# Softmax denominators of a fused attention and MoE kernel: block sums on VectorE and a 20-column product in place of a full-width product, with a newly searched order on TensorE

## The chip, the cores and the metric

The kernel runs on one core of one Trainium2 chip. TensorE (PE) multiplies, VectorE (DVE), ScalarE (ACT) and GpSimd (POOL) do the elementwise work, SyncE (SP) issues the transfers. The metric is device time in microseconds (us), the median of the runs; lower is better.

## The reference

Two stages. The first is attention with queries averaged in pairs, for 8 batches and 8 heads; its output, rearranged to 576 rows of 512 for each batch, goes into a mixture of four causal attention experts of which each row takes two.

```python
# stage 1: q, k, v are (8, 8, 1152, 64)
q_pool = q.reshape(B, H, S // 2, 2, D).mean(axis=3)
scores = scale * np.matmul(q_pool, k.transpose(0, 1, 3, 2))
attn = np.exp(scores - np.max(scores, axis=-1, keepdims=True))
attn = attn / (np.sum(attn, axis=-1, keepdims=True) + 1e-09)
attn_out = np.matmul(attn, v)
# stage 2: x is (8, 576, 512), for each of E = 4 experts, K = 2 chosen for each row
q, k, v = x @ wq[e], x @ wk[e], x @ wv[e]
scores = np.where(causal, -1e9, scale * (q @ k.transpose(0, 2, 1)))
a = np.exp(scores - scores.max(-1, keepdims=True))
a /= a.sum(-1, keepdims=True) + 1e-09
ye = a @ v @ wo[e]                # out += gate weight of (row, e) * ye
```

Both stages divide by a sum of P = exp(scores - max) over the keys. That sum is what the change touches.

## The kernel before

The 64 heads are taken in 32 pairs p, two heads side by side in 128 partitions (`HEAD[0]`, `HEAD[1]`). The 576 pooled queries of a pair are cut into two blocks of 256 and 320 (`QB`), the 1152 keys into nine chunks of 128. Scores are computed transposed: keys in the partitions, queries along the columns, so that P (`pt`, 128 x 2 heads x up to 320) is at once the right operand of the product with V.

TensorE's work comes in three kinds, each a way of splitting the array:

- A (`rows2`, line L326): two products of 64 rows each at once. The scores in four terms (qh, kh; qh, kl; ql, kh; RM, ON), and the plain products whose row maximum DVE takes (`row_max`, L573; tile PM).
- B (`cols2`, L333): two products of 64 output columns each at once, fp32. P times V into an accumulator, and the denominators. The trace keeps two records for each fp32 matmul, so one call of `cols2` is four records.
- C (`mm`, L317, and the transposes of L623): the whole array. The projections of the experts (x with WH, WL), the output product (y with OH, OL), and small ones.

The sum over the keys runs in two steps. ACT copies the first chunk's P into `sacc` (`act_first`, L342), POOL adds the other chunks elementwise (`pool_tt`, L350). What is left is a sum over 128 partitions. Before the change `g_norm` leaves it to TensorE: `cols2` with a 128 x 64 matrix of ones as the left operand writes `den`, 64 identical rows of n = 256 or 320 sums for each head. DVE then transposes `den` in 32 x 32 blocks into `rd` (L723), takes the reciprocal of one column of each block (L726, 8 or 10 numbers for each partition), multiplies by the gate weight in the expert stage (L732), and spreads the numbers back along the columns with a second block transpose (L735). `g_split` then scales the accumulator with it and splits the result into a high and a low part for the next product. There are 96 such products: 64 in stage 1 (32 pairs, two blocks), 32 in the expert stage (8 batches, two pairs of experts, two blocks).

`sacc` comes from a ring of three buffers (`NSA`), `pt` from one of 11, and all results of TensorE (scores, accumulators, `den`) from eight PSUM banks (`gen`).

The order in which instructions stand on the engines is set when the kernel is built. A planner keeps a clock for each engine, with a cost for each instruction (`emit`), and at each step takes the next piece of work from a set of generators (`f_max`, `f_st`, `f_av`, `g_norm` and others). How it chooses is steered by a row of 13 numbers out of the table `PLAN`, one row for each half pair: how long it may wait for work of the kind that is running, from which rank work is put off, how many products with V must be ready before kind B is entered, and so on. Before the change the table is 16 rows, then 8 rows five times over, then 9 rows. A generator's condition `rdy("DVE", t)` offers a step to DVE only when DVE's clock has reached the time t at which its input is due; `on(...)` gives TensorE the time itself.

Of the kernel before, what the change touches and what calls it, by code (L numbers as in the profile page):

```python
# [60 lines left out]
HEAD = [  # L61
# [16 lines left out]
]  # L78
CYCLE = [
# [8 lines left out]
]  # L88
TAIL = [
# [9 lines left out]
]  # L99
PLAN = HEAD + CYCLE * 5 + TAIL  # L100
# [61 lines left out]
def pooled_attention_then_moe_kernel(ctx: ExitStack, tc: tile.TileContext, qT, kT, vP, wall, wop, out):  # L162
# [25 lines left out]
    ones = cst.tile([128, 64], F32, name="ones")  # L188
    nc.vector.memset(ones, 1.0)
# [35 lines left out]
    r_sacc = ring("sacc", [128, 2, 320], F32, NSA)  # L225
# [10 lines left out]
    r_rd = ring("rd", [128, 320], F32, 2)  # L236
# [103 lines left out]
    def act_first(o, i, n, R, W):  # L340

        nc.scalar.activation(o, i, AF.Copy, bias=1e-9 / 128, scale=1.0)  # L342
        emit("ACT", n / 1200 + 0.083, R, W)
# [5 lines left out]
    def pool_tt(o, a, b, op, n, R, W):  # L349
        nc.gpsimd.tensor_tensor(o, a, b, op=op)  # L350
        emit("POOL", n * 0.0024 + 0.1, R, W)
# [48 lines left out]
    def on(cond, *t):  # L400
        return max((0.0,) + t) if cond else INF
# [284 lines left out]
    def f_av(p, c, hf, pt):  # L686
# [13 lines left out]
        if c == 0:  # L700
            act_first(sacc[:, :, :n], pt[:, :, :n], 2 * n, [pt], [sacc])
        else:
            pool_tt(sacc[:, :, :n], sacc[:, :, :n], pt[:, :, :n], ALU.add, 2 * n, [pt], [sacc])
# [6 lines left out]

    def g_norm(acc, sacc, n, box, gate=None):
# [4 lines left out]
        yield (lambda: on(True, r_gen.avail(), r_rd.avail(), sacc.rw), "B", den_prio)  # L716
        den, rd = r_gen.new(), r_rd.new()
        cols2(lambda r: den[r, :n], lambda j: ones, lambda j: sacc[:, j, :n], True, True, n, [sacc], [den])
        sacc.free()
        yield lambda: rdy("DVE", den.rw, r_r9.avail())  # L720

        k, r9 = n // 32, r_r9.new()
        nc.vector.transpose(rd[:, :n], den[:, :n])  # L723
        emit("DVE", n / 960 + 0.18, [den], [rd])
        o, w = (den[:, 384:384 + k], den) if gate else (r9[:, :k], r9)
        nc.vector.reciprocal(o, rd[:, :n].rearrange("p (a b) -> p a b", b=32)[:, :, 0])  # L726
        emit("DVE", 0.31 if not gate else 0.25, [rd], [w])
        rd.free()
# [295 lines left out]
    def f_mav(b, ep, qb, c, pt):  # L1024
# [18 lines left out]
        if c == 0:  # L1043
            act_first(sacc[:, :, :qn], pt[:, :, :qn], 2 * qn, [pt], [sacc])
        else:
            add = any_tt if tail_now() else pool_tt
            add(sacc[:, :, f:qn], sacc[:, :, f:qn], pt[:, :, f:qn], ALU.add, 2 * n, [pt], [sacc])
# [165 lines left out]
```

## Time and profile before

| | |
|---|---|
| median of 3 runs | 1192.66 us (1191.6 to 1193.48) |
| span of the profiled execution | 1189.9 us, first to last instruction |
| PE busy | 1151.2 us, 97% |
| POOL busy | 974.9 us, 82% |
| PE weight loads (PEld) busy | 890.1 us, 75% |
| DVE busy | 857.1 us, 72% |
| ACT busy | 703.7 us, 59% |
| DMA queue of the transfers | 18.9% of 16 engines' span |

The profiled execution has no time of its own on the page, only its span; the timed runs' median is 2.76 us above that span. Busy time is the union of an engine's instructions. TensorE's matmuls overlap in the array and their ends are modelled, so what a matmul costs the engine is read from the distance between the starts of consecutive ones in the timeline, not from its own duration.

### The profile page before, as it was taken

To read this page: it belongs to the slowest core of one execution; us is meant where nothing else is said; L and a number is where in the kernel's file an instruction comes from. 1 tells how busy PE (TensorE), PEld (TensorE's weight loads), DVE (VectorE), ACT (ScalarE), POOL (GpSimd) and SP (SyncE) were. 2 spreads that over 40 slices of the span, in tenths; PEclk is the share of its full clock that TensorE was granted. 3 is DMA by queue.
4 is the path that set the end of the run, shared out by engine and by line. 5 is a ranking of instruction groups with operands and counts; after the bars stand their busy time and mean duration, and the time that the engine had idled before them with its cause. 6 is when DMAs were issued, how large, how long until landed. Compare 5 with 4: busy or idle time off the path is not lost.

```text
span 1189.9 us, 29438 instructions
## 1 busy us (share of the span) xinstructions
PE 1151.2 (97%) x11233; PEld 890.1 (75%) x11233; DVE 857.1 (72%) x2114; ACT 703.7 (59%) x2036; POOL 974.9 (82%) x844
## 2 busy tenths in 40 slices
PE   6999999999999999999999999999999999999997
PEld 4676886778876788777886787876887677877785
DVE  7988668766776767777677676776767776577265
ACT  5676546665465655665556754566646665465624
POOL 4999978897799967999679987799797996889912
PEclk9999999999999999999999999999999999999999
DMA  5232212022212212122011221112211222200001
GB/s 159 81 103 70 62 54 68 15 70 74 62 55 60 66 48 62 55 61 97 28 42 54 86 85 29 44 48 86 78 42 35 61 66 88 61 15 9 10 28 45
DMA packets 40569, 70.30 MB, mean 59 GB/s; under 512 B 4886, under 2 KB 31724, under 8 KB 40428
## 3 DMA queue, kind: packets, MB, share of 16 engines
q1 hardware_dynamic: 40284, 68.29, 18.9%
q8 instruction: 88, 1.44, 0.5%
q14 instruction: 53, 0.43, 0.1%
q10 hardware_dynamic: 144, 0.13, 0.0%
HBM read 58.73 MB, written 9.44 MB: 57 GB/s over the span
## 4 chain that ended last, share of the span: by engine, by line
PE 60%; POOL 29%; ACT 4%; issue 3%; DVE 3%; DMA 0%; POOLq 0%; SPq 0%; ACTq 0%; DVEq 0%
POOL sacc L350 25%; PE gen L326 23%; PE gen L317 19%; PE gen L333 18%; POOL kl L350 2%; ACT pt L667 2%; POOL pt L1019 1%; DVE PM L573 1%; ACT pt L1000 1%; PE gen L623 0%; ACT sacc L342 0%; DMA qraw<-in_qT 0%; POOL gate L872 0%; DVE gen L735 0%; DVE gen L346 0%
## 5 line engine op out<-in xcount | busy, mean ns | idle before, releaser
L350 POOL TENSOR_TENSOR sacc<-sacc,pt 128x640 f32<-128x640 f32 (+4 forms) x588 | 831.0, 1418 | 123.9 <-ACT sacc L342 88.3
L573 DVE TENSOR_REDUCE PM<-gen 128x1 f32<-128x384 f32 x864 | 425.6, 550 | 168.2 <-PE gen L326 139.3
L667 ACT ACTIVATE pt<-gen 128x320 f32<-128x320 f32 (+1 forms) x1152 | 381.6, 432 | 129.5 <-PE gen L326 122.5
L333 PE MATMUL gen<-pt,v 128*64 128x320 f32 (+4 forms) x2752 | 353.4, 401 | 1.5 <-POOL pt L1019 0.3
L333 PEld LDWEIGHTS gen<-pt,v 128*64 128x64 f32 (+1 forms) x2752 | 191.2, 137 | 137.3 <-issue 9.3
L326 PE MATMUL gen<-qh,kh 64*128 64x320 f32 (+1 forms) x1152 | 215.9, 315 | 2.7 <-ACT pt L667 1.4
L326 PE MATMUL gen<-qh,kl 64*128 64x320 f32 (+1 forms) x1152 | 200.6, 298 | 0.0
L326 PE MATMUL gen<-RM,ON 64*128 64x320 f32 (+1 forms) x1152 | 194.3, 292 | 0.8 <-ACT RM L337 0.8
L326 PE MATMUL gen<-ql,kh 64*128 64x320 f32 (+1 forms) x1152 | 194.1, 292 | 0.0
L326 PE MATMUL gen<-kh,qh 64*128 64x384 f32 x768 | 158.7, 368 | 7.7 <-ACT qh L337 7.1
L326 PEld LDWEIGHTS gen<-qh,kh 64*128 64x128 f32 x1152 | 136.4, 185 | 32.1 <-issue 10.8
L326 PEld LDWEIGHTS gen<-RM,ON 64*128 64x128 f32 x1152 | 133.3, 186 | 1.2 <-ACT RM L337 1.1
L326 PEld LDWEIGHTS gen<-ql,kh 64*128 64x128 f32 x1152 | 132.7, 186 | 0.0
L326 PEld LDWEIGHTS gen<-qh,kl 64*128 64x128 f32 x1152 | 129.4, 186 | 0.0
L326 PEld LDWEIGHTS gen<-kh,qh 64*128 64x128 f32 x768 | 89.6, 187 | 38.6 <-issue 14.5
L317 PE MATMUL gen<-x,WH 128*128 128x320 f32 (+1 forms) x512 | 104.6, 299 | 0.2 <-ACT accs L337 0.2
L350 POOL TENSOR_TENSOR kl<-kraw,kh 128x384 fp32r<-128x384 f32 x96 | 95.6, 1015 | 8.9 <-ACT mqh L337 3.4
L957 DVE CUSTOM_DVE_ANT_0 gen<-gen,mqk 64x288 f32<-64x288 f32 (+4 forms) x160 | 74.7, 504 | 20.7 <-PE gen L326 19.6
L317 PEld LDWEIGHTS gen<-x,WH 128*128 128x128 f32 x512 | 81.9, 188 | 3.0 <-ACT accs L337 1.5
L333 PE MATMUL gen<-sacc,ones 128*64 128x320 f32 (+1 forms) x384 | 65.7, 423 | 14.7 <-POOL sacc L350 14.0
L337 ACT CAST x<-gen 128x256 fp32r<-128x256 f32 x64 | 25.8, 403 | 85.7 <-DVE gen L346 73.0
L317 PE MATMUL gen<-x,WL 128*128 128x320 f32 (+1 forms) x256 | 75.4, 294 | 0.0
(117 smaller groups left out, 1567.4 us busy)
## 6 DMA issues: line engine op xcount, KB each, us to landing
kraw<-in_kT SPq DMA_DIRECT2D x96, 192.0 KB
v<-in_vP SPq DMA_DIRECT2D x96, 192.0 KB
qraw<-in_qT SPq DMA_DIRECT2D x31, 576.0 KB
out<-ob SPq DMA_DIRECT2D x28, 256.0 KB
wst<-in_wall SPq DMA_DIRECT2D x8, 193.0 KB
RM<-nt SPq DMA_DIRECT2D x62, 2.5 KB
out<-ob SPq DMA_DIRECT2D x6, 128.0 KB
out<-pt SPq DMA_DIRECT2D x3, 256.0 KB
```

The lines of the kernel that those rows point to most:

```text
L317: nc.tensor.matmul(o, lhsT, rhs, start=start, stop=stop)
L326: nc.tensor.matmul(o(j), l(HEAD[j]), r(HEAD[j]), start=i == 0, stop=i == len(terms) - 1)
L333: nc.tensor.matmul(o(HEAD[j]), l(j), r(j), start=start, stop=stop)
L337: nc.scalar.copy(o, i)
L350: nc.gpsimd.tensor_tensor(o, a, b, op=op)
L573: nc.vector.tensor_reduce(pm[:, i, t:t + 1], ps[:, :384], axis=AX.X, op=ALU.max)
L667: nc.scalar.activation(pts[i][:, j, :qn], st[j][:, qn * i:qn * i + qn], AF.Exp, scale=0.0625)
L957: nc.vector.tensor_tensor_reduce(p, p, mqk[:m, 384 + m - w:384 + m], 1.0, LOW, ALU.add, ALU.max, pm[:m, j, c, i:i + 1])
L1000: nc.scalar.activation(pt_[:kn, j, f:qn], st[j][:kn, o - n:o], AF.Exp, scale=0.125)
L1019: nc.gpsimd.affine_select(out=sq, in_=sq, compare_op=ALU.is_ge, fill=0.0, base=0, pattern=[[0, 2], [1, kn]], channel_multiplier=-1)
```

## The change

First, `g_norm` no longer gives the sum over the partitions to TensorE at full width. DVE reads `sacc` once with a reduction that transposes each 32 x 32 block on the way in (`fold32`): the result `part` holds, for each group of 32 partitions, the group's sum of each query, 32 queries down the partitions and 16 or 20 columns across (8 or 10 for each head). TensorE then adds the four groups with a 128 x 64 matrix `fold` of zeros and ones, in fp32, on 8 or 10 columns for each head. The block transpose of `den` into `rd` and the ring `rd` go; the reciprocal reads `den` in PSUM. `sacc` becomes flat, so that the two heads' columns lie next to each other also in the block of 256, and is freed by DVE's fold instead of by TensorE's product. Second, the table `PLAN` is a new one of 65 rows, with no part that repeats.

```diff
-HEAD = [
-    (0.05, 0.1, 0.1, 2, 1, 1.0, 0.25, 0.02, 1, 4.5, 3.9, 4.6, 4.55),
...
-PLAN = HEAD + CYCLE * 5 + TAIL
+PLAN = [
+    (0.2, 0.3, 0.6, 6, 4, 2.0, 0.12, 0.02, 3, 4.5, 3.9, 4.6, 4.55),
...
-    ones = cst.tile([128, 64], F32, name="ones")
-    nc.vector.memset(ones, 1.0)
+    fold = cst.tile([128, 2, 32], F32, name="fold")
+    for i in range(2):
+        nc.vector.tensor_reduce(fold[:, i, :], ident.rearrange("p (g r) -> p r g", g=4), axis=AX.X, op=ALU.add)
+    fold = fold.rearrange("p a b -> p (a b)")
...
-    r_sacc = ring("sacc", [128, 2, 320], F32, NSA)
+    r_sacc = ring("sacc", [128, 640], F32, NSA)
+    r_part = ring("part", [128, 20], F32, 4)
...
-    r_rd = ring("rd", [128, 320], F32, 2)
...
+    def fold32(out, src, n, R, W):
+        nc.vector.tensor_reduce(out, src.rearrange("p a (b r) -> p a b r", r=32), axis=AX.X, op=ALU.add,
+                                apply_transpose=True)
+        emit("DVE", n / 960 + 0.12, R, W)
...
     def g_norm(acc, sacc, n, box, gate=None):
...
-        yield (lambda: on(True, r_gen.avail(), r_rd.avail(), sacc.rw), "B", den_prio)
-        den, rd = r_gen.new(), r_rd.new()
-        cols2(lambda r: den[r, :n], lambda j: ones, lambda j: sacc[:, j, :n], True, True, n, [sacc], [den])
+        yield lambda: rdy("DVE", sacc.rw, r_part.avail())
+        part, k = r_part.new(), n // 32
+        fold32(part[:, :2 * k].rearrange("p (a b) -> p a b", a=2),
+               sacc[:, :2 * n].rearrange("p (a q) -> p a q", a=2), 2 * n, [sacc], [part])
         sacc.free()
+        yield (lambda: on(True, r_gen.avail(), part.rw), "B", den_prio)
+        den = r_gen.new()
+        for j in range(2):
+            nc.tensor.matmul(den[HEAD[j], 400:400 + k], fold, part[:, j * k:j * k + k], start=True, stop=True)
+        emit("PE", 0.2, [part], [den], 0.0, "B")
+        part.free()
...
-        nc.vector.transpose(rd[:, :n], den[:, :n])
-        emit("DVE", n / 960 + 0.18, [den], [rd])
...
-        nc.vector.reciprocal(o, rd[:, :n].rearrange("p (a b) -> p a b", b=32)[:, :, 0])
-        emit("DVE", 0.31 if not gate else 0.25, [rd], [w])
-        rd.free()
+        nc.vector.reciprocal(o, den[:, 400:400 + k])
+        emit("DVE", 0.31 if not gate else 0.25, [den], [w])
```

The added lines shift the line numbers: L326, L333, L317, L350 and L573 of before are L355, L362, L346, L379 and L602 of after; the fold is L739, the small product L764.

On TensorE, about a third of the way through the program, a run of kind B opens with the denominators of one block. Before (`sacc,ones` is the full-width product, `pt,v` are products with V):

```order
L326 MATMUL gen_6488<-RM_95,ON 128x256
L326 MATMUL gen_6489<-RM_95,ON 128x256
L333 MATMUL gen_6500<-sacc_6124,ones 64x320 x2
L333 MATMUL gen_6302<-pt_6241,v_2_4642 64x192 x2
L333 MATMUL gen_6302<-pt_6266,v_2_4642 64x64 x2
L333 MATMUL gen_6515<-pt_6337,v_5721 64x256 x2
L333 MATMUL gen_6522<-sacc_6303,ones 64x320 x2
L333 MATMUL gen_6515<-pt_6338,v_5721 64x256 x2
```

The same place after (`part,fold` is the small product):

```order
L355 MATMUL gen_6485<-RM_96,ON 128x256
L355 MATMUL gen_6486<-RM_96,ON 128x256
L764 MATMUL gen_6497<-part_6432,fold 64x10 x2
L362 MATMUL gen_6507<-pt_6336,v_5669 64x256 x2
L362 MATMUL gen_6507<-pt_6337,v_5669 64x256 x2
L362 MATMUL gen_6507<-pt_6376,v_5669 64x256 x2
L362 MATMUL gen_6507<-pt_6377,v_5671 64x256 x2
L362 MATMUL gen_6507<-pt_6434,v_5671 64x256 x2
L362 MATMUL gen_6507<-pt_6435,v_5671 64x256 x2
L362 MATMUL gen_6507<-pt_6460,v_5673 64x256 x2
L362 MATMUL gen_6507<-pt_6461,v_5673 64x256 x2
L764 MATMUL gen_6541<-part_6505,fold 64x10 x2
```

The products stand at the same kind of place, inside a run of kind B, with 10 columns for each head instead of 320; the second one stands eight products with V behind the first instead of three. Over the whole program TensorE changes kind 322 times before and 357 times after.

On DVE at the same place, before: row maxima (L573), then the chain of one block from the transpose of `den` on (L723), and the next block's transpose.

```order
L573 TENSOR_REDUCE PM_98<-gen_6481 128x1
L573 TENSOR_REDUCE PM_98<-gen_6482 128x1
L723 STREAM_TRANSPOSE rd_6501<-gen_6500 128x320
L726 RECIPROCAL r_29_6507<-rd_6501 128x10
L735 STREAM_TRANSPOSE gen_6500<-r_29_6507 128x320
L346 TENSOR_TENSOR gen_6500<-accs_6327,gen_6500 128x320
L723 STREAM_TRANSPOSE rd_6523<-gen_6522 128x320
```

After, with the fold (L739) as a step of its own ahead of the chain:

```order
L602 TENSOR_REDUCE PM_99<-gen_6426 128x1
L602 TENSOR_REDUCE PM_99<-gen_6427 128x1
L739 TENSOR_REDUCE part_6432<-sacc_6253 128x20
L375 TENSOR_TENSOR qraw_6368<-qraw_6368 128x576
L771 RECIPROCAL gen_6497<-gen_6497 128x10
L776 TENSOR_TENSOR r_29_6500<-gen_6497,gs_5500 128x10
L779 STREAM_TRANSPOSE gen_6497<-r_29_6500 128x320
L375 TENSOR_TENSOR gen_6497<-accs_6321,gen_6497 128x320
L739 TENSOR_REDUCE part_6505<-sacc_6198 128x20
```

The transpose of `den` is gone, and a reduction that needs only `sacc`, that is POOL's last addition, stands in DVE's queue one or several instructions ahead of the rest of the chain; whatever DVE has behind it waits if POOL is late.

More of the change, by code (lines that the diff above doesn't have):

```diff
@@ L60 @@
 GR = 2
-HEAD = [
[16 rows of a table removed]
-]
-CYCLE = [
[8 rows of a table removed]
-]
-TAIL = [
[9 rows of a table removed]
-]
-PLAN = HEAD + CYCLE * 5 + TAIL
+PLAN = [
[65 rows of a table added]
+]
 INF = float("inf")
@@ L699, in f_av @@
               c == 0, c == NKC - 1, n, [v, pt], [acc])
[L700 to L703, printed above, removed]
+        add_up(sacc, pt, 0, n, n, c, pool_tt)
         pt.free()
@@ L709, in f_av, with add_up @@
             spawn("xfin", f_xfin(p, hf, ACC.pop((p, hf)), SACC.pop((p, hf))))
+    def fold32(out, src, n, R, W):
+        nc.vector.tensor_reduce(out, src.rearrange("p a (b r) -> p a b r", r=32), axis=AX.X, op=ALU.add,
+                                apply_transpose=True)
+        emit("DVE", n / 960 + 0.12, R, W)
+    def add_up(sacc, pt, f, n, qn, c, add):
+        s, p = sacc[:, :2 * qn].rearrange("p (a q) -> p a q", a=2)[:, :, f:], pt[:, :, f:qn]
+        if c == 0:
+            act_first(s, p, 2 * n, [pt], [sacc])
+        else:
+            add(s, s, p, ALU.add, 2 * n, [pt], [sacc])
     def g_norm(acc, sacc, n, box, gate=None):
@@ L715, in g_norm @@
         acc.free()
-        yield (lambda: on(True, r_gen.avail(), r_rd.avail(), sacc.rw), "B", den_prio)
-        den, rd = r_gen.new(), r_rd.new()
-        cols2(lambda r: den[r, :n], lambda j: ones, lambda j: sacc[:, j, :n], True, True, n, [sacc], [den])
+        yield lambda: rdy("DVE", sacc.rw, r_part.avail())
+        part, k = r_part.new(), n // 32
+        fold32(part[:, :2 * k].rearrange("p (a b) -> p a b", a=2),
+               sacc[:, :2 * n].rearrange("p (a q) -> p a q", a=2), 2 * n, [sacc], [part])
         sacc.free()
+        yield (lambda: on(True, r_gen.avail(), part.rw), "B", den_prio)
[4 more added lines that the diff above has]
+        part.free()
         yield lambda: rdy("DVE", den.rw, r_r9.avail())
-        k, r9 = n // 32, r_r9.new()
-        nc.vector.transpose(rd[:, :n], den[:, :n])
-        emit("DVE", n / 960 + 0.18, [den], [rd])
+        r9 = r_r9.new()
         o, w = (den[:, 384:384 + k], den) if gate else (r9[:, :k], r9)
-        nc.vector.reciprocal(o, rd[:, :n].rearrange("p (a b) -> p a b", b=32)[:, :, 0])
-        emit("DVE", 0.31 if not gate else 0.25, [rd], [w])
-        rd.free()
+        nc.vector.reciprocal(o, den[:, 400:400 + k])
+        emit("DVE", 0.31 if not gate else 0.25, [den], [w])
         if gate:
@@ L1042, in f_mav @@
         v32.u, v32.ue = max((v32.u, v32.ue), (vr.u, vr.ue))
[L1043 to L1047, printed above, removed]
+        add_up(sacc, pt, f, n, qn, c, any_tt if tail_now() else pool_tt)
         pt.free()
```

96 rows, old and new, of tables (CYCLE, HEAD, PLAN, TAIL) are left out of this document.

## The prediction

> **What bounds the kernel now.** I read the page's parts 1, 2 and 4 first, for which engine is full and whether it is full everywhere.
>
> ```profile
> PE 1151.2 (97%) x11233; PEld 890.1 (75%) x11233; DVE 857.1 (72%) x2114; ACT 703.7 (59%) x2036; POOL 974.9 (82%) x844
> PE   6999999999999999999999999999999999999997
> POOL 4999978897799967999679987799797996889912
> PEclk9999999999999999999999999999999999999999
> PE 60%; POOL 29%; ACT 4%; issue 3%; DVE 3%; DMA 0%; POOLq 0%; SPq 0%; ACTq 0%; DVEq 0%
> ```
>
> TensorE is busy in every slice but the first and the last, at full granted clock: time taken off its path should show. But POOL holds 29% of the chain that ended last and has nines of its own, so I cut the span into stretches: the start without expert work, one period of four pairs and a batch of experts, and a period divided finer.
>
> ```profile
> 50.00:150.00 100.00, 94.19 (x931) 71.59 (x928) 81.13 (x158) 62.84 (x180) 95.83 (x68) 1.00 0.27 81
> 579.00:722.00 143.00, 140.53 (x1394) 109.55 (x1392) 104.44 (x254) 86.48 (x251) 120.31 (x104) 1.00 0.20 60
> 624.00:708.00 84.00, 81.64 (x799) 59.73 (x796) 63.31 (x151) 53.03 (x154) 80.08 (x68) 1.00 0.23 70
> 708.00:744.00 36.00, 36.00 (x347) 29.44 (x346) 23.91 (x60) 19.59 (x55) 25.26 (x20) 1.00 0.18 47
> ```
>
> The columns are the stretch, its length, then busy time of PE, PEld, DVE, ACT and POOL. From 624 to 708 both PE (97%) and POOL (95%) are full; from 708 to 744 PE alone is. In the first 150 us POOL (96%) is fuller than PE (94%). So TensorE bounds over the whole, and POOL is close behind it in more than half of the time. DVE never passes 81%.
>
> Then the groups of the work that goes, and what waits for it:
>
> ```profile
> L333 PE MATMUL gen<-sacc,ones 128*64 128x320 f32 x192 | 35.7, 450 | 6.7 <-POOL sacc L350 6.2 <-ACT pt L667 0.2
> L333 PE MATMUL gen<-sacc,ones 128*64 128x256 f32 x192 | 30.3, 395 | 7.9 <-POOL sacc L350 7.8
> PE gen L333 <- POOL sacc L350: 14.0, 17, 1.6
> PE gen L326 <- ACT qh L337: 7.1, 2, 6.9
> DVE PM L573 <- PE gen L326: 139.3, 109, 3.9
> ```
>
> All of TensorE's idle time is 1189.9 - 1151.2 = 38.7 us. The largest item of it, 14.0 us in 17 places, is the product that is to be replaced, held up by POOL's last addition. DVE mostly waits for PE, not the other way round.
>
> **What the product costs now.** Its busy time (66 us) counts modelled ends that lie beside the next matmul, so I price it by starts, in two places of the timeline where it stands among products with V.
>
> ```profile
> 303.45 0.76 PE L333 MATMUL gen<-pt,v 128*64 128x320 f32 x4
> 304.04 0.60 PE L333 MATMUL gen<-sacc,ones 128*64 128x256 f32 x4
> 304.48 3.40 PE L333 MATMUL gen<-pt,v 128*64 128x320 f32 x24
> 307.81 0.49 PE L326 MATMUL gen<-mkh,mqh 64*128 64x512 f32 x2
> ...
> 354.95 0.76 PE L333 MATMUL gen<-sacc,ones 128*64 128x320 f32 x4 [0.67 <-POOL sacc L350]
> 355.54 0.49 PE L333 MATMUL gen<-pt,v 128*64 128x192 f32 x4
> ```
>
> With 256 columns: 304.48 - 304.04 = 0.44 us. With 320 by the columns 0.44 x 320/256 = 0.55; the place at 354.95 gives 0.59, directly behind a wait. 48 products of each width: 48 x (0.44 + 0.55) = **47.5 us**, none of it beside other TensorE work. It goes.
>
> **What the small product costs.** Two matmuls, four records, with 8 or 10 columns; no matmul so narrow is in the trace. Below: the narrowest product with V, 64 rows by 64 columns, has the group row here, and products of kind A with 128 columns follow each other like this:
>
> ```profile
> L333 PE MATMUL gen<-pt,v 64*64 64x64 f32 x64 | 5.3, 242 | 0.0
> 203.25 0.22 PE L326 MATMUL gen<-mqh,mkh 64*128 64x128 f32 x2
> 203.30 0.27 PE L326 MATMUL gen<-mqh,mkl 64*128 64x128 f32 x2
> 203.41 0.28 PE L326 MATMUL gen<-mql,mkh 64*128 64x128 f32 x2
> ```
>
> Upper bound: 5.3 us over 64 records, 16 products, 0.33 us each. Lower: two steps of two records at 0.05 to 0.11 us, say 0.06 each, 0.12 us. I take 0.2, in the middle, since both rows have more columns (which pulls down) but the first also the fp32 records of this one (which pulls up). 96 x 0.2 = 19.2 us, bounds 11.5 and 31.7. Net off TensorE: 47.5 - 19.2 = **-28.3 us** (-36.0 to -15.8).
>
> The Trainium skill, TensorE: Matmul & The Clock Gate, section Back-to-back issue gap, gives about 60 cycles, 25 ns, as the floor for up to 64 columns, and 81 ns as the sustained spacing at 128 columns, because the weight load then paces the stream. Four matmuls at the floor would be an estimated 0.10 us and 96 of them 10 us; at the sustained spacing 0.32 us and 31 us. The rows at 203.25 are already below that spacing, two at a time, and that is why I don't sum by it.
>
> **What the fold costs, and where.** It lies on DVE, and the transpose of `den` goes from there:
>
> ```profile
> L723 DVE STREAM_TRANSPOSE rd<-gen 128x320 f32<-128x320 f32 x48 | 24.5, 510 | 13.7 <-PE gen L333 13.3
> L723 DVE STREAM_TRANSPOSE rd<-gen 128x256 f32<-128x256 f32 x48 | 21.2, 441 | 24.5 <-PE gen L333 24.3
> L573 DVE TENSOR_REDUCE PM<-gen 128x1 f32<-128x384 f32 x864 | 425.6, 550 | 168.2 <-PE gen L326 139.3 <-PE gen L317 24.3
> L961 DVE TENSOR_REDUCE MPM<-gen 64x1 f32<-64x288 f32 x32 | 12.9, 442 | 0.3 <-PE gen L326 0.3
> ```
>
> Off: 24.5 + 21.2 = 45.7 us. On: the two reductions give (550 - 442)/(384 - 288) = 1.125 ns a column, so 640 columns cost 550 + 256 x 1.125 = 838 ns and 512 cost 694 ns: 48 x 1.532 = 73.5 us. No reduction in the trace transposes. Lower bound: that of 384 columns, 550 ns, 52.8 us. Upper: a transposing pass (69 ns for 64 columns, so 855 ns at 640 and 717 at 512) and a summing pass one after the other, 48 x (1.693 + 1.411) = 149 us. I take 73.5, since a block transpose here runs at about the same 1.08 ns a column as a reduction and so need not slow it. DVE goes from 857 to 885 us, 76% of a span of 1162; at the upper bound 960, 83%. DVE's waits for PE (139.3 us on one line) cover either in sum; what they don't cover is the single instruction queued behind a fold that itself waits for POOL (row maxima, and with them the banks that TensorE needs).
>
> The Trainium skill, VectorE: DVE Perf Modes, section Rules for kernel authors, speaks against the change: it calls `tensor_reduce` the slowest DVE operation, at one element a cycle, and advises restructuring. The rows agree on the rate (384 columns in 550 ns); by the rule DVE grows by the same 28 us, and it decides only if DVE is on the path, which is the slower rival below.
>
> **The waits.** TensorE's 14.0 us for POOL's last addition become waits for POOL and then for DVE's fold. The new order gives the product a somewhat later place (eight products with V between the two in front.md, against three), about what the fold takes. With everything kept the 14.0 stays, with a better place it is 0; I take half, **-7 us**, and keep 0 and -14 as ends.
>
> **The order.** 35 more changes of kind. One costs: in the timeline at 304.48, 24 records are 12 steps, 307.81 - 304.48 = 3.33 us, at 0.55/2 = 0.275 us each 3.30; the new kind's first step is then slow:
>
> ```profile
> 201.59 0.39 PE L326 MATMUL gen<-qh,kh 64*128 64x256 f32 x2
> 201.81 0.28 PE L326 MATMUL gen<-qh,kl 64*128 64x256 f32 x2
> 201.93 0.28 PE L326 MATMUL gen<-ql,kh 64*128 64x256 f32 x2
> ```
>
> 0.22 us instead of 0.12. Some 0.1 to 0.2 us with what the old kind loses; at 0.2, 35 x 0.2 = **+7 us** (+3.5 at 0.1). The Trainium skill, TensorEngine Tiling (Array Packing), section Key Properties, says that a change of tiling mode drains TensorE; the slow first step agrees.
>
> What else a new table could win or lose shows in no row; its waits are in the term above, so it gets nothing more.
>
> **Smaller edits.** The fold's constants are two reductions at the start; the one row of that shape:
>
> ```profile
> L1138 DVE TENSOR_REDUCE rep<-ident x1: 380/380/380, 47.8 to 47.8; 128x32 f32<-128x128 f32 x1
> 5.45 0.93 DVE L346 TENSOR_TENSOR qraw<-qraw 128x320 f32<-128x320 f32 x1 [0.87 <-DMA qraw<-in_qT]
> ```
>
> 2 x 0.38 = 0.76 us in front of an addition that waits 0.87 us for its transfer: nothing; without that cover 0.76 us. The reciprocal reads as many numbers as before. `sacc` is freed by a fold of 0.84 us on DVE instead of a product of 0.55 us that waits for a run of kind B; three buffers, so nothing. POOL's additions have the same sizes. No transfer is added or moved past another but in the general order, with the queues at 19%.
>
> **Sum.** -28.3 - 7 + 7 = -28.3 us on a span of 1189.9, 1161.6; the runs' median lies 2.76 us above the span, so 1192.66 - 28.3 = **1164 us**. Its own bounds: 1156 to 1172, by the price of the small product and half of the waits' ends. Chance 0.57.
>
> **Rivals.**
>
> POOL takes over. Where POOL is full TensorE's saving shortens nothing: 100 us of the start and 84 of each 143 us in seven periods, 688 of 1190. The saving then counts in the other 42%: 28.3 x 0.42 = 11.9, 1181 us. For it: 80.08 us of POOL in 84. Against: POOL has 120.31 in 143 over the period, a new order may move products with V out of the full stretch, and 4 us of slack in the 84 is more than the 2 us that the stretch would shorten. Chance 0.20.
>
> The order wins more: no wait for POOL at all (-14), the small product at its lower bound (-36), +7 for the changes: 1192.66 - 43 = 1150 us. Chance 0.15.
>
> Slower: TensorE waits for the fold. If on one product in two nothing lies between POOL's last addition and the small product, a fold of 0.77 us on average stands on the path 48 times, 36.8 us: 1192.66 - 28.3 + 36.8 = 1201 us. It decides from 28.3/96 = 0.29 us of new waiting for each product. Against: TensorE waits at all in only 17 of 96 places now. Chance 0.05.
>
> The change does not do what it says: the small product costs its upper bound and no wait goes, and POOL keeps the rest; within 0.2%, about 2.4 us, which is what a measurement of this kernel can tell from no change. Chance 0.03.
>
> **How the numbers follow.** The likeliest case gives 1164. The range 1147 to 1183 takes in the centres of the POOL rival (1181) and of the better order (1150) with some of the width of each, and leaves out their outer parts, the unchanged and the slower case, about 2 in 10. Faster 0.57 + 0.20 + 0.15 = 0.92, the same 0.03, slower 0.05.
>
> **What would show it.** Groups: the small product at 0.1 to 0.33 us by starts, no full-width one; the fold at about 0.84 and 0.69 us with DVE near 885 us; PE's busy time down by about 28 to 45 us (its rows held 66). Waits: PE for POOL's `sacc` gone, in its place PE for DVE's `part` at 7 us or less, and DVE for POOL at the fold. If POOL bounds, its share in the stretches that were full goes to 99% while PE's falls below 95%. I would be wrong if the fold took over 1.5 us, if row maxima queued behind it left TensorE without banks, or if POOL's additions grew longer beside it.

## The result, and the profile after

The changed kernel takes 1173.79 us (median of 4 runs, 1173.13 to 1174.46), the kernel before 1192.33 us in 4 runs beside it: ratio 0.984, 95% interval 0.982 to 0.986, or 18.5 us less. That lies between the likeliest case of the prediction (1164) and its POOL rival (1181), a little nearer to the second.

The page of the changed kernel, the parts that were read first of the kernel before: busy time, slices, the chain.

```profile
PE 1137.2 (97%) x11233; PEld 885.1 (75%) x11233; DVE 883.6 (75%) x2120; ACT 700.6 (60%) x2036; POOL 969.5 (83%) x839
PE   7999999999999999999999999999999999999997
POOL 4899997988789977899689985899886997979922
PEclk9999999999999999999999999999999999999999
PE 67%; POOL 20%; DVE 8%; issue 3%; ACT 2%; DMA 1%; POOLq 0%; SPq 0%; DVEq 0%; ACTq 0%
```

The span is 1172.7 us, 17.2 less. TensorE's busy time fell by 14.0 us and its idle time by only 3.2 (38.7 to 35.5): TensorE is as full as before, with less to do. In the chain POOL went from 29% to 20% and DVE from 3% to 8%.

The groups of the new work, and its waits:

```profile
L739 DVE TRANSPOSE_TENSOR_REDUCE part<-sacc 128x16 f32<-128x512 f32 (+1 forms) x96 | 73.5, 771 | 42.1 <-POOL sacc L379 41.7
L739 DVE TRANSPOSE_TENSOR_REDUCE part<-sacc x96: 669/754/847, 38.3 to 1160.9; 128x16 f32<-128x512 f32 x48, 128x20 f32<-128x640 f32 x48
DVE part L739 <- POOL sacc L379: 41.7, 38, 4.2
PE gen L764 <- DVE part L739: 9.7, 15, 1.4
PE gen L355 <- DVE PM L602: 3.2, 6, 0.9
PEld gen L355 <- DVE PM L602: 18.2, 63, 1.1
```

The folds take 73.5 us. TensorE's 14.0 us of waiting for POOL's `sacc` became 9.7 us for `part` in 15 places. DVE itself stands 41.7 us at the fold, in 38 places, until POOL's last addition is there.

The small product by starts, in the timeline where it stands between products with V:

```profile
449.10 0.44 PE L362 MATMUL gen<-pt,v 128*64 128x320 f32 x2
449.37 0.24 PE L764 MATMUL gen<-part,fold 128*64 128x8 f32 x4
449.45 0.47 PE L362 MATMUL gen<-pt,v 128*64 128x320 f32 x2
```

449.45 - 449.37 = 0.08 us. Over all of them the median is 0.11 us with 8 columns and with 10; a few take far longer, so the mean is 0.15.

**Where the time went.** For every step on TensorE (two records of kind A, four of kind B or of a product of denominators, one of C) I took the time from its start to the next step's start, and compared it with the median of steps of the same form that their own kind follows, the same medians for both kernels. What is above that median is put down to what comes next: the product (wait ahead), another kind (change of kind), or the same kind (A, B and C). The product's own time is from its start to the next start. Both kernels have the same steps of A, B and C, so the differences add up; records missing from a trace fall into the column A. Other ways to pair the records or to take the medians move the columns behind the first by up to 2 us in this row, so tenths are not to be read into them. In us:

| | product itself | wait ahead of it | changes of kind | A | B and C | sum |
|---|---|---|---|---|---|---|
| after, against before | -38.1 | -4.7 | +7.4 | +12.2 | +6.1 | -17.1 |

The product fell from 52.6 to 14.5 us. 25.7 us of what was saved with it and with its waits was spent again, all over the program: 52 more changes of kind outside the product at 0.14 us each, and A, B and C that follow each other less tightly. Some 3 us of it are clock: from 50 to 150 us TensorE was granted 1.00 before and 0.97 after.

### The profile page after: what moved, and what is told of

Read it like the earlier page. It is cut to its first block, busy times and chain, and to the rows that moved or that the text cites. A ratio compares the mean times of both kernels' runs of the same rounds, so it can differ in the third digit from the quotient of the medians.

```text
span 1172.7 us, 29459 instructions
## 1 busy us (share of the span) xinstructions
PE 1137.2 (97%) x11233; PEld 885.1 (75%) x11233; DVE 883.6 (75%) x2120; ACT 700.6 (60%) x2036; POOL 969.5 (83%) x839
## 4 chain that ended last, share of the span: by engine, by line
PE 67%; POOL 20%; DVE 8%; issue 3%; ACT 2%; DMA 1%; POOLq 0%; SPq 0%; DVEq 0%; ACTq 0%
PE gen L355 30%; PE gen L362 19%; POOL sacc L379 18%; PE gen L346 17%; DVE PM L602 3%; POOL kl L379 1%; DVE gen L1001 1%; DVE part L739 1%; ACT pt L696 1%; PE gen L764 1%; POOL pt L1063 1%; PE gen L652 0%; DMA qraw<-in_qT 0%; DVE MPM L1001 0%; DVE qraw L375 0%
## 5 line engine op out<-in xcount | busy, mean ns | idle before, releaser
L379 POOL TENSOR_TENSOR sacc<-sacc,pt 128x512 f32<-128x512 f32 (+3 forms) x583 | 821.4, 1415 | 124.0 <-ACT sacc L371 81.9
L602 DVE TENSOR_REDUCE PM<-gen 128x1 f32<-128x384 f32 x864 | 425.6, 547 | 129.6 <-PE gen L355 108.5
L362 PE MATMUL gen<-pt,v 128*64 128x320 f32 (+4 forms) x2752 | 358.7, 404 | 1.2 <-POOL pt L1063 0.8
L362 PEld LDWEIGHTS gen<-pt,v 128*64 128x64 f32 (+1 forms) x2752 | 186.5, 137 | 118.2 <-issue 11.0
L355 PE MATMUL gen<-qh,kh 64*128 64x320 f32 (+1 forms) x1152 | 224.8, 322 | 2.9 <-DVE PM L602 1.7
L355 PE MATMUL gen<-qh,kl 64*128 64x320 f32 (+1 forms) x1152 | 207.8, 300 | 0.0
L355 PE MATMUL gen<-ql,kh 64*128 64x320 f32 (+1 forms) x1152 | 199.7, 293 | 0.0
L355 PE MATMUL gen<-RM,ON 64*128 64x320 f32 (+1 forms) x1152 | 199.7, 293 | 0.0
L355 PE MATMUL gen<-kh,qh 64*128 64x384 f32 x768 | 163.7, 378 | 8.7 <-ACT qh L366 7.0
L355 PEld LDWEIGHTS gen<-qh,kh 64*128 64x128 f32 x1152 | 143.0, 186 | 37.6 <-issue 12.4
L355 PEld LDWEIGHTS gen<-RM,ON 64*128 64x128 f32 x1152 | 138.9, 187 | 0.0
L355 PEld LDWEIGHTS gen<-ql,kh 64*128 64x128 f32 x1152 | 138.6, 187 | 0.0
L355 PEld LDWEIGHTS gen<-qh,kl 64*128 64x128 f32 x1152 | 134.3, 186 | 0.0
L355 PEld LDWEIGHTS gen<-kh,qh 64*128 64x128 f32 x768 | 91.6, 188 | 46.9 <-issue 23.5
L379 POOL TENSOR_TENSOR kl<-kraw,kh 128x384 fp32r<-128x384 f32 x96 | 102.0, 1082 | 7.2 <-ACT pt L696 4.1
L739 DVE TRANSPOSE_TENSOR_REDUCE part<-sacc 128x16 f32<-128x512 f32 (+1 forms) x96 | 73.5, 771 | 42.1 <-POOL sacc L379 41.7
L346 PE MATMUL gen<-x,WH 128*128 128x320 f32 (+1 forms) x512 | 103.6, 297 | 0.0
L346 PEld LDWEIGHTS gen<-x,WH 128*128 128x128 f32 x512 | 82.1, 188 | 0.8 <-issue 0.4
L346 PE MATMUL gen<-x,WL 128*128 128x320 f32 (+1 forms) x256 | 75.6, 295 | 0.0
L1044 ACT ACTIVATE pt<-gen 128x320 f32<-128x320 f32 (+2 forms) x224 | 64.0, 388 | 17.5 <-PE gen L355 16.9
```

Source lines behind the costliest of these rows:

```text
L346: nc.tensor.matmul(o, lhsT, rhs, start=start, stop=stop)
L355: nc.tensor.matmul(o(j), l(HEAD[j]), r(HEAD[j]), start=i == 0, stop=i == len(terms) - 1)
L362: nc.tensor.matmul(o(HEAD[j]), l(j), r(j), start=start, stop=stop)
L602: nc.vector.tensor_reduce(pm[:, i, t:t + 1], ps[:, :384], axis=AX.X, op=ALU.max)
L739: nc.vector.tensor_reduce(out, src.rearrange("p a (b r) -> p a b r", r=32), axis=AX.X, op=ALU.add, apply_transpose=True)
L1044: nc.scalar.activation(pt_[:kn, j, f:qn], st[j][:kn, o - n:o], AF.Exp, scale=0.125)
```

## The experiments

Of each run the ratio to the kernel before, measured beside it, is given with its 95% interval; the differences in the table further below come from the profiled executions. The expectations speak of three theories of where the 10 us went that were forecast and did not come: W, DVE stands at the fold for POOL, with row maxima behind it; P, POOL's pace bounds; O, the new order costs time of its own.

### Does the gain belong to the product or to the table?

One part of the change at a time: the new product with the old table, and the old product with the new table.

```diff
 # after.py
-PLAN = [ ... ]                  # 65 rows
+PLAN = HEAD + CYCLE * 5 + TAIL  # 33 rows, before.py's
```

> The new denominators with the old table of 33 rows: what the product does without the new search. Theory O (the new order costs time of its own): 1164 to 1172 us, as forecast from the product alone. Theories W and P (the order was found for the product and is needed): slower than the changed kernel, 1180 to 1195, with more changes of kind on TensorE (426 in the order against 357).

Measured: 1216.11 us, ratio 1.019 (1.017 to 1.020), above both forecasts.

```diff
 # before.py, its g_norm with ones and rd
-PLAN = HEAD + CYCLE * 5 + TAIL
+PLAN = [ ... ]                  # after.py's 65 rows
```

> The kernel before with the new table: what the table does without the product. A table found for other costs should lose: 1195 to 1215 us. If the table alone brings a part of the 18.5 us (theory: the search did the work, not the product), 1180 to 1190.

Measured: 1223.78 us, ratio 1.025 (1.024 to 1.027), above both forecasts too. Each half alone loses about 2%. But neither is a clean half, since the planner makes a third order of it: with the old table and the new product the product's own time falls by 38.2 us, as in the changed kernel, while 110 more changes of kind cost 23.0 us and A 28.7. A part of that is the clock, which was granted at 0.985 in the mean: 1215.9 x 0.015 = 18 us over the whole kernel. So I also exchanged the product in the order of before as it stands: each instruction keeps its place, the small product stands where the full-width one stood, and each fold goes to DVE as soon as `sacc` is due by the planner's clock.

```diff
 # before.py
-        cols2(lambda r: den[r, :n], lambda j: ones, lambda j: sacc[:, j, :n], True, True, n, [sacc], [den])
+        issue_folds(lambda x: x[0] is sacc)       # at the latest here
+        for j in range(2):
+            nc.tensor.matmul(den[HEAD[j], 400:400 + k], fold, part[:, j * k:j * k + k], start=True, stop=True)
+        emit("PE", av_cost(n), [sacc], [den], 0.0, "B")   # the planner's cost as before
...
-        nc.vector.transpose(rd[:, :n], den[:, :n])
```

> The kernel before with its own table, every instruction in its old place, and only the denominators exchanged: the fold stands on DVE where the planner's clock says POOL is done, the small product where the full-width one stood, the transpose of den is left out. This is the product alone. If the forecast's terms hold (product -38 us by the starts measured in the changed kernel, waits unchanged): 1153 to 1160 us. If the wait at the fold gives half of it back also here (theory W): 1165 to 1178. If the product is only worth something in an order found for it: 1185 or more.

Measured: 1208.7 us, ratio 1.013 (1.012 to 1.014). The same exchange that takes 36 us from the product makes the kernel 15 us slower. TensorE's waits and page line in that run:

```profile
PE gen L742 <- DVE part L729: 32.6, 35, 1.9
DVE part L729 <- POOL sacc L361: 32.3, 34, 4.5
PE 1139.8 (94%) x11233; PEld 892.6 (74%) x11233; DVE 882.1 (73%) x2115; ACT 704.3 (58%) x2036; POOL 973.2 (81%) x844
```

TensorE waits for the fold in 35 places, where it waited for POOL in 17. Its busy time is within 3 us of the changed kernel's, its share of the span 94% instead of 97%. But the new waiting, 26.9 us by the accounting, is less than the 36.2 us that the product saved; the kernel is slower only by what follows besides, 27.7 us in changes of kind, A, B and C. The granted clock was 0.984 in the mean in place of 0.999, and 1208.2 x 0.016 = 19 us of lost clock would be the larger part of that.

### What does the fold's lateness cost?

Two kernels with the order of the changed one, instruction for instruction. In the first the fold reads a constant tile instead of `sacc`, so it waits for nobody; in the second the fold stays as it is and the small product reads the constant.

```diff
+    still = cst.tile([128, 640], F32, name="still")
+    nc.gpsimd.memset(still, 1.0)
 # first
-               sacc[:, :2 * n].rearrange("p (a q) -> p a q", a=2), 2 * n, [sacc], [part])
+               still[:, :2 * n].rearrange("p (a q) -> p a q", a=2), 2 * n, [sacc], [part])
 # second
-            nc.tensor.matmul(den[HEAD[j], 400:400 + k], fold, part[:, j * k:j * k + k], start=True, stop=True)
+            nc.tensor.matmul(den[HEAD[j], 400:400 + k], fold, still[:, j * k:j * k + k], start=True, stop=True)
```

> The changed kernel with the fold reading a constant tile of the same size instead of sacc: same order on every engine, same lengths, but DVE no longer waits for POOL's last addition, and the small product only for the fold. Leaves out the true denominators. Theory W (what was forecast and did not come, some 10 us, and the 8 us by which the small product was cheaper than summed, went into DVE waiting 41.7 us at the fold with row maxima behind it): 1152 to 1160 us. Theory P (POOL's pace bounds, the wait at the fold only shows it): within 4 us of the changed kernel, 1170 to 1174. Theory O (the new order's changes of kind and narrow places cost, not the waits): the same, 1168 to 1174.

> The changed kernel with the small product reading a constant tile instead of part: DVE still waits for POOL at the fold, TensorE waits for nobody at the product. Leaves out the true denominators. It splits theory W: if TensorE's own waits at the product (9.7 us of idle time) are what counts, 1162 to 1166 us; if the row maxima held behind the fold are, 1170 to 1174 with the fold's wait still near 42 us. Theories P and O: 1168 to 1174.

Measured: the fold that waits for nobody 1160.83 us, ratio 0.973 (0.971 to 0.974); the product that waits for nobody 1170.5, ratio 0.981 (0.979 to 0.982). Against the changed kernel that is 13 us and 3 us, the second hardly beyond what the intervals allow. The fold of the first, and what the second waits for:

```profile
L741 DVE TRANSPOSE_TENSOR_REDUCE part<-still 128x16 f32<-128x512 f32 (+1 forms) x96 | 72.8, 764 | 0.1
PE gen L766 <- DVE part L741: 1.8, 2, 1.1
```

```profile
DVE part L741 <- POOL sacc L381: 49.1, 42, 4.6
PE gen L357 <- DVE PM L604: 5.1, 9, 1.0
PEld gen L357 <- DVE PM L604: 21.1, 66, 1.3
```

With the product free, the wait ahead of it shrinks by 12.6 us, but A grows by 6.7 and B and C by 3.3: TensorE runs past the product and meets row maxima that stand on DVE behind the fold (5.1 us for PM instead of 3.2, weight loads 21.1 instead of 18.2). These waits grew by 1.9 and 2.9 us, at most half of the 10 that come back; the clock, 0.995 in the mean in place of 0.997, is another 2, and the rest was not traced. Most of the lateness is paid either at the product or behind it; what ends it is a fold that need not wait. The same pair in the old order:

```diff
 # the kernel before with the product exchanged
-            nc.tensor.matmul(den[HEAD[j], 400:400 + k], fold, part[:, j * k:j * k + k], start=True, stop=True)
+            nc.tensor.matmul(den[HEAD[j], 400:400 + k], fold, still[:, j * k:j * k + k], start=True, stop=True)
```

> The old order with the new product once more, but the small product reads a constant of 20 columns instead of part: the fold still stands on DVE and still waits for POOL, TensorE waits for no one at the product. Leaves out the true denominators. With the product waiting this order took 1208.7 us, 32.6 us of TensorE's idle time at the product and a granted clock of 0.984. If that wait, and the clock with it, is what the old order lacked: 1155 to 1168 us, clock back to 0.997 or more. If DVE held up at the fold costs as much (row maxima behind it): 1180 to 1200 us, with the clock still low.

Measured: 1202.2 us, ratio 1.008 (1.006 to 1.010). 37.7 us leave the place ahead of the product and 21.5 come back in A; the clock, 0.990 in the mean, comes back only in part:

```profile
DVE part L731 <- POOL sacc L363: 58.3, 54, 4.9
PE gen L339 <- DVE PM L586: 15.3, 15, 1.8
PE gen L346 <- DVE PM L586: 5.9, 5, 1.2
```

### Is the fold too early on DVE, or too long?

Too early: each fold is issued two DVE instructions later, everything else in its place.

```diff
     def fold32(out, src, n, R, W):
-        nc.vector.tensor_reduce(out, ..., apply_transpose=True)
+        go_ = lambda: nc.vector.tensor_reduce(out, ..., apply_transpose=True)
         emit("DVE", n / 960 + 0.12, R, W)
+        pending.append([2, go_, W[0]])     # issued after two more on DVE, at the latest before its product
```

> The changed kernel with each fold issued two DVE instructions later (or just ahead of its product, if that comes first), all else in the same place: POOL gets 0.5 to 1 us more time before DVE stands still. Theory W: DVE's wait for POOL falls from 41.7 to 25 us or less, and the time to 1165 to 1171 us. If TensorE then waits for the fold instead: 1173 to 1178, with a larger wait at the product.

Measured: 1202.43 us, ratio 1.007 (1.006 to 1.009), far above both forecasts.

```profile
L750 DVE TRANSPOSE_TENSOR_REDUCE part<-sacc 128x16 f32<-128x512 f32 (+1 forms) x96 | 73.6, 768 | 5.7 <-POOL sacc L389 5.3
PE gen L777 <- DVE part L750: 27.4, 29, 2.8
```

DVE now stands 5.3 us for POOL instead of 41.7, and TensorE 27.4 us for `part` instead of 9.7. The standing on DVE is the cheaper side: 36 us less of it cost 29 us of the end.

Too long: in place of the fold a short instruction from the same `sacc` to the same `part`, first a copy of 16 or 20 columns, then a plain reduction of 32 or 40.

```diff
-        nc.vector.tensor_reduce(out, src.rearrange("p a (b r) -> p a b r", r=32), axis=AX.X, op=ALU.add,
-                                apply_transpose=True)
 # first
+        nc.vector.tensor_copy(out, src[:, :, :n // 64])
 # second
+        nc.vector.tensor_reduce(out, src[:, :, :n // 32].rearrange("p a (b r) -> p a b r", r=2), axis=AX.X, op=ALU.add)
```

> The changed kernel with a copy of 8 or 10 columns for each head in place of the fold, same order: leaves out the sum over the blocks. DVE still waits for POOL, but the fold's 73.5 us fall to some 20. If the fold's own length counts (DVE's load, or the step between POOL and the product): 1160 to 1168 us. If only POOL's lateness does (theory W): 1169 to 1174.

> The changed kernel with a plain reduction of 32 or 40 columns in place of the fold of 512 or 640, same order; leaves out most of the sum. In the run with a copy the copy of 16 or 20 columns lasted as long as the fold (773 ns), so that run did not shorten it. This one has one input in SBUF and no copy: about 0.2 us each, 19 us in place of 73.5. If the fold's length counts: 1158 to 1168 us. If only POOL's lateness does: 1169 to 1174.

Measured: with the copy 1176.6 us, ratio 0.986 (0.984 to 0.987), no different from the changed kernel; with the reduction 1165.49, ratio 0.977 (0.976 to 0.978).

```profile
L739 DVE COPY part<-sacc x96: 160/794/1546, 38.3 to 1163.0; 128x16 f32<-128x16 f32 x48, 128x20 f32<-128x20 f32 x48
```

```profile
L739 DVE TENSOR_REDUCE part<-sacc x96: 158/185/196, 38.1 to 1151.6; 128x16 f32<-128x32 f32 x48, 128x20 f32<-128x40 f32 x48
```

The columns behind the count are the shortest, median and longest duration in ns. The copy was a miss: meant to be short, it lasted as long as the fold. The reduction was short, 17 us in all instead of 73.5, and brought 8 us: of DVE's 56 us about one in seven reaches the end.

### Does POOL's pace eat the gain?

POOL's additions on half the columns, in the changed kernel and in the kernel before.

```diff
-        nc.gpsimd.tensor_tensor(o, a, b, op=op)
+        if len(o.shape) == 3:
+            h = o.shape[2] // 2
+            nc.gpsimd.tensor_tensor(o[:, :, :h], a[:, :, :h], b[:, :, :h], op=op)
+        else:
+            nc.gpsimd.tensor_tensor(o, a, b, op=op)
```

> The changed kernel with POOL's additions on half of the columns, in the same order: leaves out half of the sums. POOL's 821 us of additions fall to about 440. Theory P (POOL's pace bounds): 1150 us or less, more than the removal of the fold's wait alone gives. Theory W: about what the fold that reads a constant gives, 1152 to 1162, since POOL is then never late. Theory O: 1168 to 1174.

> The kernel before with POOL's additions on half of the columns, in the same order: leaves out half of the sums. It shows what POOL held back before. By the 14.0 us of TensorE's idle time in front of the full-width product: 1176 to 1182 us. If POOL held TensorE back in other ways too (P buffers, 11 of them): 1165 to 1175. If not at all: 1190.

Measured: 1148.95 us, ratio 0.963 (0.961 to 0.964), for the changed kernel, and 1171.07, ratio 0.981 (0.980 to 0.983), for the kernel before.

```profile
PE 1129.4 (98%) x11233; PEld 884.8 (77%) x11233; DVE 856.5 (75%) x2120; ACT 697.2 (61%) x2036; POOL 611.5 (53%) x839
```

```profile
PE 1147.1 (98%) x11233; PEld 894.0 (76%) x11233; DVE 834.3 (71%) x2114; ACT 700.1 (60%) x2036; POOL 615.2 (53%) x844
```

POOL's 358 us less bring 25 us after the change and 22 before, and with the intervals these are not apart. With POOL's additions halved in both, the change is worth 1171.07 - 1148.95 = 22.1 us, where it is worth 18.5 with the whole: POOL costs both kernels about the same; it took some 4 us of the gain, barely clear of the noise, where the prediction's POOL rival has it take 28.3 - 11.9 = 16.4.

### How much of it is this one order?

The planner is told 0.01 us more for each fold; the program is otherwise that of the changed kernel.

```diff
-        emit("DVE", n / 960 + 0.12, R, W)
+        emit("DVE", n / 960 + 0.13, R, W)
```

> The changed kernel with the planner's cost of the fold 0.01 us higher: another order by a hair's breadth (387 changes of kind instead of 357), no other change. It shows how much of the time hangs on this very order. If the table is fitted to one order: 1180 us or more. If any similar order does: 1172 to 1177.

Measured: 1225.83 us, ratio 1.027 (1.025 to 1.029), 52 us above the changed kernel with the same instructions on the data. Over a third of that is one place; windows of 10 us (busy time of PE, PEld, DVE, ACT, POOL, then the granted clock) and ACT's next instruction there:

```profile
740.00:750.00 10.00, 7.62 (x19) 3.79 (x19) 9.85 (x40) 0.00 (x0) 9.53 (x8) 0.62 0.01 2
750.00:760.00 10.00, 8.29 (x25) 5.24 (x25) 9.93 (x25) 0.00 (x0) 0.46 (x1) 0.50 0.01 2
760.00:770.00 10.00, 10.00 (x67) 5.95 (x69) 5.57 (x13) 0.71 (x2) 0.63 (x1) 0.69 0.00 0
767.65 0.37 ACT L366 COPY accs<-gen 128x256 f32<-128x256 f32 x1 [28.83 <-PE gen L362]
```

The order puts the row maxima of experts and of a pair of heads back to back there. DVE is full, ACT has nothing for 28.8 us, the clock goes to half, and TensorE starts 111 records in 30 us; at the mean of the changed kernel, 11233 records in 1172.7 us, they take 11.6 us.

### All differences side by side

By the accounting of the first section, in us:

| kernel, against | product itself | wait ahead of it | changes of kind | A | B and C | sum |
|---|---|---|---|---|---|---|
| fold waits for nobody, after | -2.4 | -11.1 | +0.1 | +1.1 | -0.5 | -12.8 |
| product waits for nobody, after | -0.8 | -12.6 | +0.5 | +6.7 | +3.3 | -2.9 |
| fold two later, after | +2.9 | +24.7 | -1.0 | +0.4 | -0.2 | +26.8 |
| short reduction, after | -1.1 | -6.5 | -0.7 | -1.1 | +0.3 | -9.1 |
| half additions, after | -3.1 | -12.4 | -2.7 | -6.0 | -0.6 | -24.8 |
| half additions, before | -2.0 | -16.6 | +0.2 | +0.2 | -1.9 | -20.1 |
| product alone in the old order, before | -36.2 | +26.9 | +1.9 | +10.2 | +15.6 | +18.4 |
| the same, product waits for nobody, product alone | +5.2 | -37.7 | +1.6 | +21.5 | +1.3 | -8.1 |
| old table, new product, before | -38.2 | -0.1 | +23.0 | +28.7 | +12.6 | +26.0 |
| new table, old product, before | -0.6 | -9.4 | +14.6 | +25.8 | +2.1 | +32.5 |
| cost nudged, after | +4.7 | +5.3 | +12.8 | +19.0 | +10.6 | +52.4 |

## Why the prediction was right, and where not

**The product** (-28.3) was mis-sized in both of its halves, to the same side. The full-width product measured 52.6 us by starts, not 47.5: the medians are 0.48 and 0.59 us, where 0.44 and 0.55 came from one place that was faster than most. The 0.59 us at 354.95 that the prediction set aside as standing behind a wait was the usual price. The small one measured 14.5, not 19.2; with a median of 0.11 us and a mean of 0.15 it lies near the lower bound of 0.12, and the row that it was nearest to was that of kind A at 203.25, not the 64-column product that had pulled the estimate up. Together -38.1, past the term's own lower end of -36.0. The sentence on the Trainium skill's floor (TensorE: Matmul & The Clock Gate, Back-to-back issue gap) would have given 0.10 us for four matmuls, and the trace, with 0.11 us in the median, agrees with that and not with the sustained spacing.

**The fold** was right: 73.5 us forecast and measured, by width 841 and 701 ns where 838 and 694 were forecast, DVE at 883.6 us against 885. Beside the price of a plain reduction, no time for the block transpose inside it shows. Its cover held for the most part: taking 56 of the 73.5 us away, with the short reduction, moves the end by 8.

**The waits** (-7): -4.7 ahead of the product, and TensorE's wait for `part` is 9.7 us where 7 or less was given as the sign. The size was about right. The mechanism behind it was told too simply: the prediction named the instruction behind a fold that waits for POOL as what DVE's spare time doesn't cover, but priced nothing there. The pair of kernels in which fold or product waits for nobody shows that it is for the most part the same lateness, 13 us in all, taken at the product as long as the product waits and behind it (10 of 13 us, at most half of them in waits for row maxima) when it does not.

**The changes of kind** (+7): +7.4, by two errors that cancel. 52 more instead of 35, since a border beside a product was counted before and is in the product's own time here; and 0.14 us each instead of 0.2.

**The order, "it gets nothing more"**, is the step that failed. A, B and C follow each other less tightly by 18.3 us, and by the accounting that is why the time is 1173.8 and not 1164; the product's extra 9.8 us made up for half of it. That a mis-sized product and a missing term had opposite signs is luck: without it the time would have stood at the upper end of the range. What a table can lose was taken as zero because no row showed it. The runs show its size: with tables or costs that were not searched for together with the product, A alone lost 19 to 29 us (the two halves of the change, the nudge). A part of that is clock, 0.985 in the mean with the old table and 0.980 with the nudge, but with the new table and the old product it was 0.995, and A lost 25.8 us.

The term was also wrong in kind. The table was treated as an addition to the product's change, with a price of its own. But the product alone, in the old order, is 15 us slower: 26.9 us of new waiting ahead of it, 0.28 us for each of 96, and another 27.7 us in the rest of TensorE's steps, of which up to 19 are clock. The waiting is what the rival "TensorE waits for the fold" names; its deciding point was put at 0.29 us and its time at 1201; measured 1208.7. The waiting alone stays just below that point, and it is with the clock, which the rival did not price, that the product loses. It was given 0.05 because TensorE waited for POOL in only 17 of 96 places. But that told how late POOL was for the product without a fold of 0.77 us between the two; with the fold between, TensorE waits in 35 places. What the new table did is to bring +26.9 down to -4.7 and the clock from 0.984 to 0.997; from the product alone in the old order to the changed kernel is 1208.7 - 1173.8 = 35 us. Whether a table searched anew for the old product would have gained something too was not tried; the new table was found with the new product.

**The POOL rival** came nearer in time than the likeliest case, 7 us off against 10, but it is not the cause. Its sign, POOL near 99% and PE below 95% in the full stretches, is not there; the two stretches of the prediction, after:

```profile
50.00:150.00 100.00, 97.07 (x983) 73.77 (x983) 85.62 (x165) 65.83 (x192) 94.07 (x67) 0.97 0.29 90
579.00:722.00 143.00, 140.67 (x1410) 111.36 (x1409) 106.34 (x256) 87.24 (x253) 121.63 (x106) 1.00 0.20 61
```

PE went from 94% to 97% in the first, a part of it at the lower clock of 0.97, where POOL is down from 96% to 94%, and both are as before in the second. With POOL's additions halved both kernels gain about alike.

**Still open** is what makes A 12.2 us longer. By the same accounting about 8 of them lie at the plain products of the row maxima (kh, qh) and 3 at the first of the four score terms (qh, kh), and TensorE's weight loads wait more for the row maxima, 18.2 us in 63 places now; before it was

```profile
PEld gen L326 <- DVE PM L573: 7.7, 32, 0.5
```

It isn't the fold's lateness, since the 12.2 us stay when the fold waits for nobody (+1.1 on top), nor its length, since only 1.1 of them go with the short reduction; 6.0 of them go when POOL is faster. Of the nudged order's 52 us, the clock of 0.980 is 1224.7 x 0.020 = 24 us, 21 more than the changed kernel's; the rest was not followed up.

## What to carry to other kernels

When work moves from the full engine to one with room, price the new link in the chain as well as the work: here 36 us came off TensorE, and without a new order the wait for POOL and then DVE took 27 us of it back and the rest, with a lower clock in it, another 28. A wait taken away at one consumer of an engine that works its queue in order turned up here for the most part further on, so make the producer early rather than the consumer patient. And when the order is searched for one program, undoing half of a change measures another order: keep the order fixed and exchange the instruction to learn what the instruction is worth.

## What the hardware showed that was not expected

A copy of 16 or 20 columns on DVE, from `sacc` to `part` while POOL adds, took between 160 and 1546 ns, 773 in the mean; a plain reduction that reads 32 or 40 columns of the same tile took 158 to 196. The Trainium skill (SBUF — State Buffer, Who interferes with whom) says that a copy can take the port pair that DVE shares with GpSimd and is then blocked for a whole instruction, while `tensor_reduce` never contends on trn2. The two rows agree, though no row shows the ports: POOL's additions take 1418 ns in the mean in the run with the copy, and the copy's longest time is about one of them (1386 ns) above its shortest.

The granted clock fell behind places where TensorE waits, and stayed down a while. In the kernel with the product alone in the old order:

```profile
core 0: 1208.2 us, clock 0.984
500.00:510.00 10.00, 7.46 (x74) 4.75 (x72) 8.22 (x20) 6.45 (x19) 9.77 (x10) 0.87 0.25 95
790.00:800.00 10.00, 7.43 (x79) 4.75 (x77) 8.30 (x20) 6.56 (x20) 9.76 (x10) 0.87 0.33 116
800.00:810.00 10.00, 9.81 (x81) 6.18 (x79) 6.39 (x16) 2.69 (x9) 9.40 (x9) 0.79 0.00 0
```

Two waits of 0.7 and 1.9 us ahead of products, at a busy share of 75% in the 10 us, came with 0.87 in both places, and with 0.79 in the 10 us behind the second. They don't always do it: the same two waits, 0.71 and 1.86 us, stand at 359 and 362 us of the same run, and from 350 to 370 us the granted clock is 1.00. Nor does more waiting as such: with the fold two later TensorE waits 27.4 us for `part`, and the mean clock is 0.997 as in the changed kernel. A mean of 0.984 is 1208.2 x 0.016 = 19 us of clock, against 1172.7 x 0.003 = 3.5 after the change: by these rows a wait on TensorE may cost more than its own length.
